# Mirrored filter rows by a DRAM scratch buffer in a spectral filter and token MLP kernel

## The chip, the cores and the metric

The kernel runs on one core of a Trainium2 chip. The metric is the device time of one execution in microseconds; the median of several runs is compared. The engines named below are TensorE (PE, with its weight loads PEld), VectorE (DVE), ScalarE (ACT) and SyncE (SP), whose queue issues nearly all DMA transfers. A DMA transfer is spread over up to 16 DMA engines.

## What is computed

Two branches work on the same input x (2048 rows of 512) and are mixed by a gate per row. Branch A is a two-dimensional Fourier filter: transform, product with a complex weight W of 2048 x 257, back transform. Branch B is a layer norm and an MLP over the rows.

```python
def _A_ref(x, w_r, w_i):
    X = rfft2(x.astype(float32))            # S = 2048 rows, D = 512
    X = X * (w_r + 1j * w_i)                # (2048, 257) each
    return irfft2(X, s=(S, D)).astype(bfloat16)

def _B_ref(x, w1, b1, w2, b2):
    h = _layernorm(x)
    u = gelu(einsum("bsd,sf->bdf", h, w1) + b1)          # F = 1792
    return transpose(einsum("bdf,fs->bds", u, w2) + b2)

g = sigmoid((x * gate_w).sum(-1, keepdims=True))
out = g * A + (1 - g) * B
```

## The kernel before

The kernel is one stream of tasks. `Plan` holds each task with its engine, an estimated duration, what it reads and writes, and a priority. `Plan.order()` runs through the tasks once, on the host, with a clock of its own: at each moment every engine takes, of its tasks that are ready by that clock, the one with the lowest priority number. A DMA task is charged its issue time, then 1.0 us, then its bytes at 388 KB a us, then 0.9 us to land; it waits for the landing of the eighth DMA task before it, and SP is held to 5 us before the end of what it has issued. The order that comes out is emitted as it stands, so each engine of the chip runs a fixed order of its own; only semaphores decide when.

The MLP branch fills PE. L705 (`m1`) multiplies h by w1 in 14 column tiles of F: tiles 0 to 6 from `wa`, 7 to 10 and 11 to 13 from two `wb` buffers, over 16 row tiles each. L721 on ACT is the gelu. L1011 (`m2`) multiplies by w2, which is loaded into `wa` and `wb` once their last w1 tile is used; L1017 on ACT and L1024, L1030 on DVE put the output together.

The Fourier branch is woven in between. L554 to L557 and L653 are its forward matrix products, copied out of PSUM by ACT (L560, L660). DVE does the butterflies: L585 to L598 (`radix4`) and L669 to L677 (`tb2`), each L653 group for half of the second block needing L597 and L598 of that block. L828 multiplies by the filter `W`, L833 to L846 combine; L890 to L898 and L967 to L970 on PE are the way back.

`W` is a tile [128, 2 components, 2 blocks `lt`, 4, 2, 258]. Index 0 of the last but one dimension holds rows of the weight in rising order, index 1 the mirrored rows, in falling order over the partitions. For the real and the imaginary component in turn, `ld_W` (L433) issues 16 SP loads:

- four into `wt` (L439 to L442), which hold the rows of block 0 to be mirrored, in rising order;
- four for block 1, L444, each 128 rows whose source is read as 4 groups of 32, each group backwards;
- four of 32 partitions each, then two for block 0 (63 and 64 partitions), one row of partition 0 and the row `wn`.

Each row is 257 bfloat16 values, 514 bytes. All these DMAs are recorded under L306, the helper `dma`. The four `wb` loads of w1's last columns are issued between the two components.

The `wt` rows are then turned on PE: `wf` (L754) multiplies the permutation `flip` by two of them at a time into a PSUM bank (L757), and ACT copies the result into `W` (L761, 512 columns at a time). The last column, 256, is turned for all at once by L767 and copied by L770. `flip` is also used by L685 for a bias.

`wprep` (L775 to L781) on DVE halves one row of `W` and forms sums of its end columns. It has priority 1, needs all of `W`, and every reader of `W` comes behind it. DVE's butterflies around it have priorities 2.5 to 3.3.

SP's DMAs use eight semaphores in turn: an issue waits until the eighth DMA before it has landed. The loads of w2 stand on SP behind the filter's.

Of the kernel before, what the change touches and what calls it, by code (L numbers as in the profile page):

```python
# [13 lines left out]
BF16 = mybir.dt.bfloat16  # L14
F32 = mybir.dt.float32

P = 128
# [5 lines left out]
L = 256  # L23
WL = 258
# [108 lines left out]
class Plan:  # L133
# [11 lines left out]
    def add(self, eng, dur, emit, reads=(), writes=(), prio=0.0, alloc=(), free=(), nbytes=0, after=(), late=0.0):  # L145
        t = Task()
        t.late = late
        t.eng, t.dur, t.emit, t.prio = eng, dur, emit, prio
        t.alloc, t.free, t.nbytes = tuple(alloc), tuple(free), nbytes
        t.users, t.end, t.ready = [], None, 0.0  # L150
        deps = set(after)
        for k in reads:
            if k in self.last_w:
                deps.add(self.last_w[k])
            self.readers.setdefault(k, []).append(t)
        for k in writes:
            if k in self.last_w:
                deps.add(self.last_w[k])
            deps.update(self.readers.get(k, ()))
            self.last_w[k] = t  # L160
            self.readers[k] = []
        deps.discard(t)
        t.deps = deps
        self.tasks.append(t)
        return t
# [73 lines left out]
def tt(n):  # L239
    return 0.07 + n / 1920.0  # L240
# [10 lines left out]
def act(n, ptr=0):  # L251
    return 0.065 + 0.09 * ptr + n / 1200.0


def mm(*ns):
    return sum(max(n, 120) / 2400.0 + 0.0025 for n in ns)
# [8 lines left out]
def kernel(  # L265
# [14 lines left out]
    V, A, T = nc.vector, nc.scalar, nc.tensor  # L280
# [6 lines left out]
    w2v = B_w2.rearrange("(t f) s -> f t s", f=P)  # L287

    pool = ctx.enter_context(tc.tile_pool(name="sb", bufs=1))
    psum = ctx.enter_context(tc.tile_pool(name="ps", bufs=1, space=bass.MemoryType.PSUM))  # L290
    NES = 2

    def sb(shape, dt, tag, bufs=1):
        return pool.tile(shape, dt, tag=tag, name=tag, bufs=bufs)

    def ps(shape, dt, tag, bufs):
        return psum.tile(shape, dt, tag=tag, name=tag, bufs=bufs)
# [4 lines left out]
    add = pl.add  # L302
    t = {}

    def dma(out_ap, in_ap, eng=None):
        (eng or nc.sync).dma_start(out=out_ap, in_=in_ap)  # L306

    def alloc_first():
        t["eps"] = sb([P, 1], F32, "eps")
        V.memset(t["eps"][:], 1e-5)  # L310
        t["x"] = sb([P, 4, 4, D], BF16, "x")
        t["h"] = sb([P, 4, 4, D], BF16, "h")
        t["X"] = sb([P, 2, 4, 2, 4, P], BF16, "X")
        t["B"] = sb([P, 2, 4, 4, L], BF16, "B")
        t["xp"] = sb([P, 8192], BF16, "xp")
        t["warm"] = t["xp"][:, 0:D]
        V.memset(t["warm"], 0.0)  # L317
        t["s9"] = sb([P, D], BF16, "s9")
        t["b1b"] = sb([P, P], BF16, "b1b")
        t["b2h"] = sb([P, 4, 4], BF16, "b2h")  # L320
        for k in ("s9", "b1b"):
            V.memset(t[k][:], 0.0)
        t["st"] = sb([P, 4096], BF16, "st")
        t["gl"] = sb([P, NFT, D], BF16, "gl")
        t["W"] = sb([P, 2, 2, 4, 2, WL], BF16, "W")
        t["wn"] = sb([1, 2, WL], BF16, "wn")
        t["ta"] = sb([P, 4, 640], BF16, "rot")
        t["wt"] = sb([P, 2, 4, WL], BF16, "wt")
        t["wpm"] = sb([P, 2, 2, 4, 2], F32, "wpm")
        t["sp"] = sb([P, 4, 2, 4], F32, "sp")  # L330
        t["sd"] = sb([P, 2, 2, 2, 4], F32, "sd")
        t["fx"] = sb([P, 4, 2, 4], F32, "fx")
        t["c0"] = sb([P, 2, 4, 2, 2], F32, "c0")
        t["cm"] = sb([P, 4, 4, 2], F32, "cm")
        t["ce"] = sb([P, 2, 4, 2, 2], F32, "ce")
        for name, shape in (("stats", [P, NJ, nc.vector.BN_STATS_DIM]), ("mv", [P, NJ, nc.vector.BN_AGGR_DIM]),
                            ("rstd", [P, NJ]), ("nmr", [P, NJ]), ("glog", [P, NJ]), ("g", [P, NJ]), ("omg", [P, NJ]),
                            ("ombb2", [P, NJ]), ("b1f", [P, NFT])):
            t[name] = sb(shape, F32, name)

    a0 = add("SP", 0.01, alloc_first, writes=["warm", "xs", "eps"], prio=-9)
# [88 lines left out]

    wsrc = (A_w_r, A_w_i)

    def ld_W(comp):  # L433
        v = wsrc[comp].rearrange("(e c k) l -> c e k l", e=4, k=4)
        z = wsrc[comp].rearrange("(v u w) l -> w u v l", v=4, u=2)

        def emit():
            W, u = t["W"][:, comp], t["wt"][:, comp]
            dma(u[64:127, :, 0:257], v[65:128, :, 0, :])  # L439
            dma(u[0:64, :, 0:257], v[64:128, :, 2, :])  # L440
            dma(u[127:128, 0:2, 0:257], z[0:1, 1, 2:4, :])
            dma(u[127:128, 3:1:-1, 0:257], z[0:1, 0, 0:4:3, :])  # L442
            for e in range(4):
                dma(W[:, 1, e, 1, 0:257], v[:, 3 - e, 3, :].rearrange("(o i) l -> o i l", o=4)[:, ::-1])  # L444
            for o in range(4):
                dma(W[32 * o:32 * o + 32, 1, :, 0, 0:257], v[96 - 32 * o:128 - 32 * o, :, 1, :])
            dma(W[1:64, 0, :, 0, 0:257], v[1:64, :, 0, :])
            dma(W[64:128, 0, :, 0, 0:257], v[0:64, :, 2, :])
            dma(W[0:1, 0, :, 0, 0:257].rearrange("w (u v) l -> w u v l", u=2), z[0:1, :, 0:2, :])
            dma(t["wn"][:, comp, 0:257], wsrc[comp][1024:1025, :])  # L450
        return emit

    for comp in range(2):
        add("SP", 12.3, ld_W(comp), writes=[("W", comp), ("wt", comp)], prio=17 + 8 * comp, nbytes=300000, after=[a0])
        if comp == 0:
            load_wb(1)

# [14 lines left out]
    for r in range(4):  # L472
# [3 lines left out]
        for b, qs in enumerate(groups):  # L476
            js = [4 * q + r for q in qs]
            xb = [xk[q] for q in qs]
            g = (r, b)
# [5 lines left out]
            for j in js:  # L485
# [10 lines left out]
                if j in ASTAT:  # L496
# [4 lines left out]
                    after=[rect[0, 0]] if j == 4 else ())  # L501
# [23 lines left out]
            for j in js:  # L525
                if j in HACT:
                    add("ACT", 0.71, lambda j=j: A.activation(t["h"][:, j // 4, j % 4, :], t["x"][:, j // 4, j % 4, :], ActF.Identity,  # L527
                                                                  bias=t["nmr"][:, j:j + 1], scale=t["rstd"][:, j:j + 1]),
                        reads=xb + [("rstd", *g)] + mvk, writes=[("h", j)], prio=-0.5 + 0.1 * r)
# [19 lines left out]
        for dq in range(4):  # L549
            def fa(r=r, dq=dq):  # L550
# [8 lines left out]
                free=["xf"] if dq == 3 else ())  # L559
            add("ACT", act(512), lambda r=r, dq=dq: A.copy(xe(r)[:, :, :, dq, :], t["pa", r, dq][:]),  # L560
                reads=[("pa", r, dq)], writes=[("X", r, dq)], prio=0, free=["fa"])
# [69 lines left out]
    for lt in (0, 1):  # L631
        pr = 3.0 + 0.1 * lt
# [3 lines left out]
        if lt == 0:  # L636
            add("DVE", 0.15, lambda: V.tensor_copy(t["X"][:, 0, :, :, :, 0], t["fx"][:]), reads=["fx"],
                writes=[("Z", 0, 0), ("Z", 0, 1)], prio=3.0)
# [76 lines left out]
    for n, (ft, j) in enumerate(order):  # L715
# [4 lines left out]
        if last:  # L720
# [3 lines left out]
                free=[bank]))  # L724
# [21 lines left out]

    add("SP", 0.2, ld_ti, writes=["ti"], prio=39, nbytes=754176, after=[pl.last_w["pa", r, dq] for r in range(4) for dq in range(4)])

    for comp in range(2):
        for lt in (0,):  # L750
            for a in range(2):
                tag = ("fa", "fb")[a]

                def wf(comp=comp, lt=lt, a=a, tag=tag):  # L754
                    pw = t["pw", comp, lt, a] = ps([P, 2, L], F32, tag, 2)
                    for i in range(2):
                        T.matmul(pw[:, i], lhsT=t["flip"][:], rhs=t["wt"][:, comp, 3 - 2 * a - i, 0:L], start=True, stop=True)  # L757
                add("PE", mm(256, 256), wf, reads=[("wt", comp), "flip"], writes=[("pw", comp, lt, a)], prio=5, alloc=[tag])

                def wfe(comp=comp, lt=lt, a=a):  # L760
                    A.copy(t["W"][:, comp, lt, 2 * a:2 * a + 2, 1, 0:L], t["pw", comp, lt, a][:])  # L761
                add("ACT", act(512), wfe, reads=[("pw", comp, lt, a)], writes=[("W~", comp, lt)], prio=3, free=[tag])

    def wfn():
        pw = t["pwn"] = ps([P, 4, 2], F32, "fa", 2)
        for e in range(4):
            T.matmul(pw[:, e], lhsT=t["flip"][:], rhs=t["wt"][:, :, 3 - e, 256], start=True, stop=True)  # L767
    add("PE", mm(*[4] * 4), wfn, reads=[("wt", 0), ("wt", 1), "flip"], writes=["pwn"], prio=5, alloc=["fa"])
    wtk = [("W~", comp, 0) for comp in range(2)]
    add("ACT", 0.3, lambda: A.copy(t["W"][:, :, 0, :, 1, 256], t["pwn"][:].rearrange("p e k -> p k e")),  # L770
        reads=["pwn"], writes=wtk, prio=3, free=["fa"])

    pbk = [("pb", lt, e, c) for lt in range(2) for e in range(4) for c in range(2)]

    def wprep():  # L775
# [3 lines left out]
        pv = [pm[:, i].rearrange("p a e k -> p (a e) k") for i in range(2)]  # L779
        V.tensor_add(pv[0], ends[0][:, :, 0], ends[0][:, :, 1])  # L780
        V.tensor_sub(pv[1], ends[1][:, :, 0], ends[1][:, :, 1])  # L781
    add("DVE", 0.8, wprep, reads=[], writes=[("W", 0), ("W", 1), "wpm"] + wtk, prio=1)


    for lt in range(2):
# [37 lines left out]
        for comp in range(2):  # L823
            def mul(lt=lt, comp=comp):
                xs = xph(0).rearrange("p (k c l) -> p k c l", k=8, c=2)
                o = (xph(1) if comp == 0 else t["st"][:]).rearrange("p (k c l) -> p k c l", k=8, c=2)
                w = t["W"][:, comp, lt].rearrange("p e s l -> p (e s) l")[:, :, None, 0:L].to_broadcast([P, 8, 2, L])
                V.tensor_mul(o, xs, w)  # L828
            add("DVE", tt(4096), mul, reads=["xs", ("W", comp), ("W~", comp, lt)], writes=[("pp", "st")[comp]], prio=pr)

        def comb(lt=lt):
            y, pp, qq = (v.rearrange("p (k c l) -> p k c l", k=8, c=2) for v in (xph(0), xph(1), t["st"][:]))
# [246 lines left out]
```

## Time and profile before

| what | value |
|---|---|
| median of 3 runs | 127.81 us (127.77 to 128.35) |
| the profiled execution | 127.68 us |
| its span, first to last instruction | 125.9 us |
| PE busy | 120.5 us, 96% of the span |
| DVE busy | 113.8 us, 90% |
| ACT busy | 81.0 us, 64% |
| DMA moved | 23.12 MB, mean 184 GB/s |
| granted TensorE clock | 1.0 throughout |

The span is cut into 40 slices of 3.15 us. A digit is the busy share of a slice in tenths:

```profile
PE   6899999999999999999999999999999999999991
ACT  0973689699999999999420004722299999952200
DMA  1999999994459946799999900000000000006541
GB/s 57 305 371 358 382 365 358 348 315 86 117 119 288 268 86 162 210 413 411 410 408 407 389 25 0 5 0 0 3 0 0 0 5 0 0 21 229 200 180 44
```

In a timeline, a row is start, duration, engine (SPq is SP's queue), line, operation, the tiles written and read, and how many were merged; an idle time before it and what ended it stand in brackets. In the list of waits, a row is the waiting engine and line, what it waited for, and the total in us, the number of waits and the longest. A window row is its bounds and length, the busy time of PE, PEld, DVE, ACT and POOL with the number of instructions, the granted clock, the mean busy share of the 16 DMA engines and GB/s. The trace also holds a landing mark for each DMA engine that takes part in a transfer.

### The profile page before, as it was taken

The page shows a single profiled execution, that of the slowest core. Times are in us where ns is not written, and L with a number is a line of the kernel's source. Part 1 is how long each engine was busy: PE and PEld are TensorE (multiplying, and loading weights), DVE is VectorE, ACT ScalarE, POOL GpSimd, SP SyncE. Part 2 cuts the span into 40 slices and gives each one's busy share as a digit, 9 for nine tenths or more (in the row PEclk, how much of TensorE's full clock was granted, in tenths as well). Part 3 has the DMA queues.
Part 4 walks back from the last instruction along what each step waited for, and adds up shares of the span by engine and source line. Part 5 has one row for each costly group of instructions (what it writes and reads, how often), then busy time and mean ns, then how long its engine had stood idle before and what let it go on. Part 6 is the DMA issues. An engine that isn't in the chain of part 4 may idle for free.

```text
span 125.9 us, 2138 instructions
## 1 busy us (share of the span) xinstructions
PE 120.5 (96%) x743; PEld 68.8 (55%) x756; DVE 113.8 (90%) x273; ACT 81.0 (64%) x165; POOL 0.2 (0%) x4
## 2 busy tenths in 40 slices
PE   6899999999999999999999999999999999999991
PEld 2344555555655476644445555555577767655590
DVE  2699999999999999999999999999988999999651
ACT  0973689699999999999420004722299999952200
POOL 0000000000000000000000000000000000000000
PEclk9999999999999999999999999999999999999999
DMA  1999999994459946799999900000000000006541
GB/s 57 305 371 358 382 365 358 348 315 86 117 119 288 268 86 162 210 413 411 410 408 407 389 25 0 5 0 0 3 0 0 0 5 0 0 21 229 200 180 44
DMA packets 18219, 23.12 MB, mean 184 GB/s; under 512 B 2190, under 2 KB 15904, under 8 KB 18208
## 3 DMA queue, kind: packets, MB, share of 16 engines
q1 hardware_dynamic: 17616, 22.36, 52.6%
q10 hardware_dynamic: 592, 0.62, 1.6%
q8 instruction: 6, 0.10, 0.3%
q14 instruction: 5, 0.04, 0.1%
HBM read 20.86 MB, written 2.10 MB: 182 GB/s over the span
## 4 chain that ended last, share of the span: by engine, by line
PE 73%; DMA 17%; SPq 7%; issue 1%; DVE 0%
PE acc L1011 32%; PE acc L705 20%; DMA wa<-in_B_w_dram 9%; SPq L306 7%; PE fb L1011 5%; DMA wt<-in_A_w_r_dram 5%; DMA x<-in_A_x_dram 3%; PE fb L653 2%; PE fa L653 2%; PE fa L890 2%; PE fb L890 1%; PE fb L705 1%; PE fa L967 1%; PE fb L967 1%; PE fa L1011 1%
## 5 line engine op out<-in xcount | busy, mean ns | idle before, releaser
L705 PE MATMUL acc<-h,wb 128*128 128x512 bf16 x108 | 25.9, 379 | 0.1
L1011 PE MATMUL acc<-gl,wb 128*128 128x512 bf16 (+1 forms) x94 | 23.9, 371 | 0.2
L1011 PE MATMUL acc<-gl,wa 128*128 128x512 bf16 (+1 forms) x97 | 23.8, 371 | 0.1
L1017 ACT ACTIVATE x<-acc,ombb,omg 128x512 bf16<-128x512 f32 x12 | 9.1, 782 | 21.2 <-PE acc L1011 21.2
L1011 PEld LDWEIGHTS <-wa 128*128 128x128 bf16 x126 | 13.5, 113 | 9.9
L1011 PEld LDWEIGHTS <-wb 128*128 128x128 bf16 x126 | 13.3, 113 | 9.3
L705 PE MATMUL acc<-h,wa 128*128 128x512 bf16 x62 | 17.3, 379 | 0.1
L705 PEld LDWEIGHTS <-wb 128*128 128x128 bf16 x112 | 10.7, 98 | 10.6
L705 PEld LDWEIGHTS <-wa 128*128 128x128 bf16 x112 | 10.3, 98 | 10.7 <-DMA wa<-in_B_w_dram 0.8
L487 DVE BATCH_NORM_STATS2 stats<-x 128x6 f32<-128x512 bf16 x14 | 9.5, 679 | 2.1 <-DMA x<-in_A_x_dram 2.0
L560 ACT CAST xp<-fa 128x512 bf16<-128x512 f32 x16 | 9.1, 581 | 1.8 <-PE fa L557 1.8
L735 ACT ACTIVATE x<-x 128x512 bf16<-128x512 bf16 x16 | 10.2, 691 | 0.0
L721 ACT ACTIVATE gl<-acc,b1f 128x512 bf16<-128x512 f32 x11 | 7.9, 718 | 3.2 <-PE acc L705 3.2
L705 PE MATMUL fb<-h,wa 128*128 128x512 bf16 x31 | 9.5, 379 | 0.1
L527 ACT ACTIVATE h<-x,nmr,rstd 128x512 bf16<-128x512 bf16 x11 | 8.4, 808 | 1.1 <-DMA wb<-in_B_w_dram 0.8
L705 PE MATMUL fa<-h,wa 128*128 128x512 bf16 x16 | 5.9, 378 | 0.7 <-DVE h L521 0.6
L653 PEld LDWEIGHTS <-X 128*128 128x128 bf16 x64 | 4.7, 98 | 2.1
L974 ACT ACTIVATE B<-fb,g 128x512 bf16<-128x512 f32 x8 | 5.7, 713 | 0.0
L974 ACT ACTIVATE B<-fa,g 128x512 bf16<-128x512 f32 x8 | 5.6, 705 | 0.1
L660 ACT CAST X<-fb 128x512 bf16<-128x512 f32 x8 | 5.1, 634 | 0.0
L660 ACT CAST X<-fa 128x512 bf16<-128x512 f32 x8 | 5.0, 620 | 0.0
L356 PE MATMUL fa<-xp 128*128 128x512 bf16 x10 | 3.8, 549 | 1.2 <-DVE xp L317 1.2
(169 smaller groups left out, 232.7 us busy)
## 6 DMA issues: line engine op xcount, KB each, us to landing
wb<-in_B_w_dram SPq DMA_DIRECT2D x11, 512.0 KB
wa<-in_B_w_dram SPq DMA_DIRECT2D x7, 512.0 KB
wa<-in_B_w_dram SPq DMA_DIRECT2D x2, 896.0 KB
wb<-in_B_w_dram SPq DMA_DIRECT2D x4, 384.0 KB
out_dram<-x SPq DMA_DIRECT2D x3, 512.0 KB
x<-in_A_x_dram SPq DMA_DIRECT2D x2, 512.0 KB
wa<-in_B_w_dram SPq DMA_DIRECT2D x2, 448.0 KB
rot<-dft_ti SPq DMA_DIRECT2D x1, 768.0 KB
```

What stands on the lines that cost most here:

```text
L306: (eng or nc.sync).dma_start(out=out_ap, in_=in_ap)
L487: V.bn_stats(out=t["stats"][:, j, :], in_=t["x"][:, j // 4, j % 4, :])
L527: add("ACT", 0.71, lambda j=j: A.activation(t["h"][:, j // 4, j % 4, :], t["x"][:, j // 4, j % 4, :], ActF.Identity, bias=t["nmr"][:, j:j ...
L560: add("ACT", act(512), lambda r=r, dq=dq: A.copy(xe(r)[:, :, :, dq, :], t["pa", r, dq][:]), reads=[("pa", r, dq)], writes=[("X", r, dq)], ...
L653: T.matmul(pb[:, k % 2, k // 2], lhsT=t["X"][:, lt, EX[e], c, k, :], rhs=tbl(k, c), start=True, stop=True)
L660: A.copy(t["X"][:, lt, EX[e]].rearrange("p c j l -> p (c j l)").rearrange("p (h c g b) -> p h c g b", h=2, c=2, b=2)[:, :, c], t["pb", lt, ...
L705: T.matmul(t["u", ft][:], lhsT=w[:, j // 4, j % 4, c * P:(c + 1) * P], rhs=t["h"][:, j // 4, j % 4, :], start=(j == jorder[0]), stop=(j == ...
L721: gelus.append(add("ACT", act(512, 1) , lambda ft=ft: A.activation(t["gl"][:, ft, :], t["u", ft][:], ActF.Gelu_apprx_tanh, bias=t["b1f"][: ...
L735: A.activation(t["x"][:, q, r, :], t["x"][:, q, r, :], ActF.Copy, accum_out=t["glog"][:, 4 * q + r:4 * q + r + 1])
L974: A.activation(eo_v(p)[:, n], t["i3", j][:], ActF.Copy, scale=t["g"][:, j:j + 1])
L1011: T.matmul(t["y", j, m][:, cs], lhsT=w[:, o, 512 * q + r:512 * q + 512:4], rhs=t["gl"][:, ft, cs], start=(ft == 0), stop=(ft == NFT - 1))
L1017: A.activation(tbuf(j).rearrange("p h d -> p (h d)"), t["y", j, 0][:], ActF.Identity, bias=t["ombb2"][:, j:j + 1], scale=t["omg"][:, j:j + 1])
```

## The change

The mirrored rows no longer pass through `wt`, PE and ACT. For each component, `ld_flip` issues two copies from the weight in DRAM into scratch buffers in DRAM, `fe` (4 x 128 rows) and `fo` (16 x 32 rows), each with its second dimension read backwards. `ld_nat` issues the loads in rising order, ten for each component, among them two single rows that need no turning. `ld_mir` reads the scratch buffers back into `W` with three loads for each component. The task durations given to the planner are 1.1 us for `ld_flip` (with 700,000 bytes), 5.5 for `ld_nat` (300,000) and 1.6 for `ld_mir` (500,000); by priority, SP's order is both `ld_flip`, `ld_nat` of the first component, the four `wb` loads, `ld_nat` of the second, both `ld_mir`, then w2. The tile `wt` and the tasks `wf`, `wfe` and `wfn` (L749 to L771) go, which the diff below leaves out; `wprep` waits for the four loads' tasks.

```diff
+    dram = ctx.enter_context(tc.tile_pool(name="dram", bufs=1, space=bass.MemoryType.DRAM))
...
-        t["wt"] = sb([P, 2, 4, WL], BF16, "wt")
...
-    def ld_W(comp):
+    def ld_flip(comp):
+        ev = wsrc[comp].rearrange("(e m w) l -> w e m l", e=4, w=2)[0, :, P:2 * P, :]
+        od = wsrc[comp].rearrange("(g i k) l -> k g i l", i=32, k=4)[3]
+
+        def emit():
+            fe = t["fe", comp] = dram.tile([4, P, 257], BF16, tag=f"fe{comp}", name=f"fe{comp}")
+            fo = t["fo", comp] = dram.tile([16, 32, 257], BF16, tag=f"fo{comp}", name=f"fo{comp}")
+            dma(fe[:], ev[:, ::-1])
+            dma(fo[:], od[:, ::-1])
+        return emit
+
+    def ld_nat(comp):
         v = wsrc[comp].rearrange("(e c k) l -> c e k l", e=4, k=4)
         z = wsrc[comp].rearrange("(v u w) l -> w u v l", v=4, u=2)
 
         def emit():
-            W, u = t["W"][:, comp], t["wt"][:, comp]
-            dma(u[64:127, :, 0:257], v[65:128, :, 0, :])
-            dma(u[0:64, :, 0:257], v[64:128, :, 2, :])
-            dma(u[127:128, 0:2, 0:257], z[0:1, 1, 2:4, :])
-            dma(u[127:128, 3:1:-1, 0:257], z[0:1, 0, 0:4:3, :])
-            for e in range(4):
-                dma(W[:, 1, e, 1, 0:257], v[:, 3 - e, 3, :].rearrange("(o i) l -> o i l", o=4)[:, ::-1])
+            W = t["W"][:, comp]
             for o in range(4):
                 dma(W[32 * o:32 * o + 32, 1, :, 0, 0:257], v[96 - 32 * o:128 - 32 * o, :, 1, :])
             dma(W[1:64, 0, :, 0, 0:257], v[1:64, :, 0, :])
             dma(W[64:128, 0, :, 0, 0:257], v[0:64, :, 2, :])
             dma(W[0:1, 0, :, 0, 0:257].rearrange("w (u v) l -> w u v l", u=2), z[0:1, :, 0:2, :])
+            dma(W[0:1, 0, 0:2, 1, 0:257], z[0:1, 0, 0:4:3, :])
+            dma(W[0:1, 0, 3:1:-1, 1, 0:257], z[0:1, 1, 2:4, :])
             dma(t["wn"][:, comp, 0:257], wsrc[comp][1024:1025, :])
         return emit
 
+    def ld_mir(comp):
+        def emit():
+            W, fe, fo = t["W"][:, comp], t["fe", comp], t["fo", comp]
+            m = fe[:].rearrange("e (p two) l -> two p e l", two=2)
+            dma(W[:, 1, ::-1, 1, 0:257], fo[:].rearrange("(e o) i l -> (o i) e l", e=4))
+            dma(W[1:64, 0, ::-1, 1, 0:257], m[1, 0:63])
+            dma(W[64:128, 0, ::-1, 1, 0:257], m[0, 0:64])
+        return emit
+
+    FL = (16, 16.1)
     for comp in range(2):
-        add("SP", 12.3, ld_W(comp), writes=[("W", comp), ("wt", comp)], prio=17 + 8 * comp, nbytes=300000, after=[a0])
+        add("SP", 1.1, ld_flip(comp), writes=[("flp", comp)], prio=FL[comp], nbytes=700000, after=[a0])
+    for comp in range(2):
+        add("SP", 5.5, ld_nat(comp), writes=[("W", comp)], prio=17 + 8 * comp, nbytes=300000, after=[a0])
+        add("SP", 1.6, ld_mir(comp), reads=[("flp", comp)], writes=[("W~", comp)], prio=26 + comp, nbytes=500000)
         if comp == 0:
             load_wb(1)
...
-    add("DVE", 0.8, wprep, reads=[], writes=[("W", 0), ("W", 1), "wpm"] + wtk, prio=1)
+    add("DVE", 0.8, wprep, reads=[], writes=[("W", 0), ("W", 1), ("W~", 0), ("W~", 1), "wpm"], prio=1)
```

## The prediction

> **What bounds the kernel now.** I read the page first (busy times, slices, chain of waits), then the timelines of DVE, PE and SyncE's queue (SP) around the changed work, then SP's waits and a few windows.
>
> ```profile
> PE 120.5 (96%) x743; PEld 68.8 (55%) x756; DVE 113.8 (90%) x273; ACT 81.0 (64%) x165; POOL 0.2 (0%) x4
> DVE  2699999999999999999999999999988999999651
> PE 73%; DMA 17%; SPq 7%; issue 1%; DVE 0%
> ...
> 24.90 2.56 SPq L306 DMA_DIRECT2D wt<-in_A_w_r_dram  x4
> 27.95 7.55 SPq L306 DMA_DIRECT2D W<-in_A_w_r_dram  x11
> 36.01 2.62 SPq L306 DMA_DIRECT2D wb<-in_B_w_dram  x4
> 41.27 8.55 SPq L306 DMA_DIRECT2D W<-in_A_w_i_dram  x11
> 50.40 3.30 SPq L306 DMA_DIRECT2D wa<-in_B_w_dram  x7
> ...
> SPq L306 <- DMA wb<-in_B_w_dram: 4.4, 4, 1.5
> ...
> 31.60:32.60 1.00, 1.00 (x11) 0.81 (x10) 1.00 (x2) 1.00 (x3) 0.00 (x0) 1.00 0.22 58
> ...
> 46.68 0.68 DVE L591 TENSOR_TENSOR X<-xp 128x1024 bf16<-128x1024 bf16 x1
> 47.55 0.69 DVE L669 TENSOR_TENSOR B<-X 128x1024 bf16<-128x1024 bf16 x1 [0.18 <-ACT X L660]
> 48.83 0.68 DVE L597 TENSOR_TENSOR X<-st 128x1024 bf16<-128x1024 bf16 x1
> 57.46 0.41 DVE L777 TENSOR_SCALAR W<-W 1x1028 bf16<-1x1028 bf16 x1
> ...
> 38.65 0.38 PE L757 MATMUL fa<-wt,flip 128*128 128x256 bf16 x2
> 53.02 0.38 PE L757 MATMUL fa<-wt,flip 128*128 128x256 bf16 x2
> ```
>
> TensorE sets the end (96% busy), but DVE is packed too: one slice after another at 9. Both run a fixed order, so a wait put into one of them in mid kernel is not filled by later work. SP is not free either: from 24.9 to 50.3 us it does nothing but issue filter loads, with the four `wb` loads between.
>
> **How an order comes to be.** The planner fixes every engine's order by its own due times; the chip then waits in that order. I take from it only where DVE's `wprep` (L777, L780, L781), which needs the whole filter, is put. Its clock can be laid on the trace: it lets the first turning matmul go 0.15 + 0.9 + 300000/388e3 + 1.0 = 2.82 us after `ld_W`'s 12.3 us of issue. The trace has it at 38.65, so the planner's `ld_W` began at 38.65 - 15.1 = 23.5; from the second (53.02) it is 37.9, and 23.5 + 12.3 + 4 x 0.5 = 37.8. The two marks agree.
>
> With the new costs from 23.5: flips 1.1 each, but SP is also held to 5 us before the planner's transfers end (at most 23.5 + 5 = 28.5 beforehand, and 1.8 more for each 700,000 bytes: 32.1), so 27.1; plain loads 5.5, 32.6; `wb` 2.0, 34.6; second plain loads 40.1; mirror reads 1.6 each, 43.3; then 1.0 + 1.29 + 0.9: due at 46.5. `wprep` has priority 1 against 2.5 and 3 of its neighbours, so it goes into DVE's next gap: behind L591, which ends at 47.3, ahead of L669 and L597. Before, it stood behind work that ended at 57.4.
>
> **What the chip does with SP's new queue.** An SP load waits until the eighth before it has landed: in the trace the first turned load is issued at 27.95 after a landing mark at 27.94, the second at 29.96 (29.94), and in the second group at 44.00 (43.98). That is the 4.4 us in the row of waits. The plan charges the new loads 0.55 us each and no such wait; the old 12.3 us for 16 was 0.77 each.
>
> Cost of a scratch row: no DRAM to DRAM copy is in the trace. Nearest rows: the old turned loads L444, 128 rows of 514 bytes whose source is 4 x 32. While they alone run, 0.22 of 16 engines are busy (last window line): 4 engines. Two of them land 1.1 us apart, so 32 rows an engine cost 1.1 us, 34 ns a row. Rows written to DRAM at the end (512 bytes, L306 stores) take 27 ns, rows read into SBUF 28 ns. The lower bound is that both overlap: 34 ns; the upper that they add, 28 + 27 and the same gap of 6 ns: 61 ns. I take 34, since the read rows already include a write.
>
> How many engines: `fo` is 16 x 32 on both sides. `fe` is 4 x 128, and the row with an outer size of 4 ran on 4 engines, so I take 4: 128 rows an engine, 4.4 us; `fo` 32 rows, 1.1 us. The other bound is 16 engines: 1.1 us for all four.
> By the Trainium skill, page "DMA: Bandwidth & Descriptors", section "Why a DMA increments its semaphore by 16 and not by 1", the number of engines is the largest up to 16 that divides the slowest dimension of both sides. By that rule `fe` gets 4 too, as the 0.22 suggests.
>
> Now in order. A load on idle engines (the first `o` load, issued by 32.30) has its first marks at 33.72: 1.4 us to land. The low four engines come free at 28.3 at the latest (old `wt` rows there landed by 30.47, less 1.4 and 28 rows, 0.95 us). Landings: fe0 28.3 + 4.4 + 1.4 = 34.1, fo0 35.2, fe1 39.6, fo1 40.7. The four `o` loads go out by 31.7 as the turned ones did. The fifth plain load waits for fe0 (34.1), the sixth for fo0 (35.2), the seventh for fe1 (39.6), the eighth for fo1 (40.7); two more end at 42.4, against 32.6 in the plan. `wb` 2.6 us (row of 36.01): 45.0. Second plain loads: four by 47.0; the next four wait for the `wb` loads, which before landed 3.4 (first) to 6.9 us (last) after their issue ended: 50.1 to 51.9 for the last, then 1.6: 51.7 to 53.5. Six mirror reads at 0.53: 54.9 to 56.7. Landing 1.4 + 16 rows x 34 ns: 56.8 to 58.6, middle 57.7.
>
> **The sum.**
> - DVE waits at `wprep` from 47.3 to 57.7: +10.4. Behind it stand L669 and L597/L598; L598 feeds the last four L653 groups (51.00 to 52.5 in the chain), and PE, in order, stops there, about 3.5 us after DVE and just as long. Behind that stand all of L1011 and ACT's copies L660. So the wait counts once.
> - Turning matmuls: 4 x 0.22 + 0.08 us of the chain (pieces at 38.81, 39.03, 53.18, 53.40, 53.84) = 0.96 off PE. Those before the stall (0.44) vanish in it; -0.52.
> - ACT copies L761, L770: 0.59 + 0.59 + 0.70 + 0.70 + 0.34 = 2.9 us, -0: ACT is in no piece of the chain. The weight loads of `flip` run under matmuls, -0. `wprep` itself is moved: 0.
> - SP: 32 loads become 30. First `wa` load of w2 at about 55.9 instead of 50.4. The cover is the stall, which moves L1011's start (64.35) by 10. Without it: seven loads of 512 KB at some 410 GB/s (the slices' rate there) take 9 us and land at about 66.4, 2 us of PE waiting.
> - Bytes: 1.05 MB more, while the DMA row of the slices stands at 4 to 7 tenths for half of 28 to 53 us: 0.
>
> 127.68 (profiled execution: span 125.9 and 1.8 around it) + 10.4 - 0.5 = 137.6. The median of the runs shown, 127.81, is 0.13 higher; I leave the forecast at 137.6.
>
> **Rivals.**
> 1. `fe` runs on 16 engines. Then all flips have landed by about 35.3 (slowest engine free at 29.5, 4 x 1.1 + 1.4), plain loads end at 36.7, `wb` 39.3, second plain loads 46.0 to 47.8, mirror reads landed 51.1 to 52.9. Stall 4.7: 131.9. For: no row shows such a copy. Against: the 0.22.
> 2. A DRAM to DRAM row costs 61 ns. fe 7.8, fo 2.0: fo1 lands 8.6 later, stall 19: 146.2. For: nothing here both reads and writes DRAM. Against: 512-byte rows to DRAM at 27 ns.
> 3. Not slower: `wprep` finds its filter there. Place: L777 on DVE. It decides at W's last landing against DVE's turn: if the turn comes 10.4 us later than I work out (the plan puts `wprep` where it was, 57.4), or the mirror rows land by 47.3 (16 engines for `fe`, no wait for a `wb` load: 24.9 + 30 x 0.53 = 40.8 is SP's floor, plus the wait at 29.96 and 2 us to land: 47 to 48). Price: 0.5 to 0.96 gained, 126.7 to 127.2; a wait of up to 1 us makes it no change. For: DVE waited nowhere for the filter before. Against: two marks that agree on the planner's clock, and the waits at 27.95, 29.96 and 44.00.
> 4. The copy doesn't do what it says, by being lowered in small pieces of more packets. It would show as rival 2 or beyond; I count it there.
>
> **How the numbers follow.** Forecast (134 to 142, from landings at 54 to 62) 0.48; rival 1 and stalls partly made good (129 to 134) 0.20; rivals 2 and 4 (142 to 150) 0.17; rival 3 0.15, of which 0.11 faster and 0.04 the same. No change means within 0.5%, 0.64 us, about what a measurement of this kernel can tell. Slower: 0.48 + 0.20 + 0.17 = 0.85. The range 130 to 146 leaves out rival 3 and about a third of the long tail, 0.2. Cases of both signs exist, but the likeliest's own 134 to 142 lies on one side.
>
> **What would show it.** In the changed profile: L777 on DVE near 47, not 57, as it is issued behind L591, with an idle time of some 10 us before it, ended by a DMA into W; the same on PE before a group of L653 near 51; SP rows with gaps before the fifth and the seventh plain load; the DMA busy share near 4 of 16 while the scratch copies run. No turning matmuls, no copies to W on ACT. The landing of fe0 against fo0 gives the row price and the engines. I am wrong if `wprep` runs near 57, or with no idle time before it; if the idle time is there but PE's is much shorter, the step that passes DVE's wait on to PE is wrong.

## The result, and the profile after

The change makes the kernel slower: 144.32 us median of 6 runs (142.21 to 145.29) against 127.79. The ratio of 1.121, with a 95% interval of 1.113 to 1.129, is that of the fast runs alone (142.21, 143.52 and 144.28), the other three being over 1.5% above the fastest. The profiled execution took 142.21 us with a span of 140.4; before, 127.68 and 125.9.

Line numbers shift: the helper of all DMAs is now L307; L591 became L611, L597 L617, L669 L689, L653 L673, L705 L725, L1011 L1007, and `wprep` (L777, L780, L781) is L773, L776, L777.

Page of the changed kernel: busy time of the engines, the slices (40 of 3.5 us), the chain of waits.

```profile
PE 122.7 (87%) x744; PEld 68.9 (49%) x744; DVE 113.5 (81%) x273; ACT 79.2 (56%) x160; POOL 0.2 (0%) x4
PE   6899999999999960007999999999999999999991
DVE  1799999999999401039969999999997999999941
PEclk9999999999999998555699999999999999999999
DMA  3999999953772993999999290000000000005441
PE 52%; DMA 26%; SPq 17%; DVE 2%; issue 1%; DVEq 0%
```

Busy times are nearly those of before; the span is longer because DVE stands still for most of 47 to 62 us and PE from 51 to 64 us, where the rows fall to 0. The granted clock falls to half in the same place. In the chain, PE's share went from 73% to 52%, DMA's and SP's grew from 24% to 43%.

The timeline of SP's queue in the changed kernel:

```profile
24.64 0.75 SPq L307 DMA_DIRECT2D fe<-in_A_w_r_dram  x1
25.44 4.20 SPq L307 DMA_DIRECT2D fo<-in_A_w_r_dram  x1
29.69 0.84 SPq L307 DMA_DIRECT2D fe<-in_A_w_i_dram  x1
30.57 4.20 SPq L307 DMA_DIRECT2D fo<-in_A_w_i_dram  x1
34.81 7.72 SPq L307 DMA_DIRECT2D W<-in_A_w_r_dram  x9
43.03 2.62 SPq L307 DMA_DIRECT2D wb<-in_B_w_dram  x4
45.70 7.17 SPq L307 DMA_DIRECT2D W<-in_A_w_i_dram  x9
53.37 0.65 SPq L307 DMA_DIRECT2D W<-fo  x1
54.07 1.55 SPq L307 DMA_DIRECT2D W<-fe  x2
55.66 0.62 SPq L307 DMA_DIRECT2D W<-fo  x1
56.33 1.44 SPq L307 DMA_DIRECT2D W<-fe  x2
57.87 3.77 SPq L307 DMA_DIRECT2D wa<-in_B_w_dram  x7
```

The mirror reads begin at 53.37, when the old queue had already issued all its filter loads and six of the first seven weight loads of w2 (the seventh at 53.27). W2's first load goes out at 57.87 instead of 50.40. By the landing marks the last mirror read is there at 62.01; the last filter load of before landed at 52.02.

The timelines of DVE and of PE in the changed kernel, in brackets the idle time before the instruction and what ended it:

```profile
46.68 0.69 DVE L611 TENSOR_TENSOR X<-xp 128x1024 bf16<-128x1024 bf16 x1
53.88 0.42 DVE L773 TENSOR_SCALAR W<-W 1x1028 bf16<-1x1028 bf16 x1 [6.51 <-DMA W<-in_A_w_i_dram]
59.40 0.18 DVE L776 TENSOR_TENSOR wpm<-W 128x16 f32<-128x16 bf16 x1 [5.10 <-DMA W<-fo]
62.09 0.19 DVE L777 TENSOR_TENSOR wpm<-W 128x16 f32<-128x16 bf16 x1 [2.51 <-DMA W<-fe]
62.19 0.69 DVE L689 TENSOR_TENSOR B<-X 128x1024 bf16<-128x1024 bf16 x1
...
50.19 1.24 PE L725 MATMUL acc<-h,wb 128*128 128x512 bf16 x5
64.21 0.61 PE L673 MATMUL fa<-tb,X 128*128 128x128 bf16 x4 [12.78 <-DVE X L617]
66.06 4.20 PE L725 MATMUL acc<-h,wb 128*128 128x512 bf16 x12
```

`wprep` now runs right behind L611, ahead of L689 and L617, and waits three times: 6.51 + 5.10 + 2.51 = 14.1 us. PE stops at 51.43 and waits 12.78 us for L617. Then it works at half speed for a while, as a window of the changed kernel shows (bounds and length, busy time and count of PE, PEld, DVE, ACT and POOL, granted clock, DMA share, GB/s):

```profile
64.20:69.20 5.00, 4.99 (x24) 2.76 (x25) 5.00 (x17) 2.26 (x5) 0.00 (x0) 0.52 1.03 410
```

A clock of 0.52 over 5.0 us is 2.4 us of work not done. The profiled executions differ by 142.21 - 127.68 = 14.5 us: 12.8 us of PE's waiting, 2.4 of slow clock, less 0.96 of turning matmuls that are gone, make 14.2; 0.3 stays unassigned.

### The profile page after: what moved, and what is told of

It reads as the page before. It is cut to its first block, busy times and chain, and to the rows that moved or that the text cites. A ratio compares the mean times of both kernels' runs of the same rounds, so it can differ in the third digit from the quotient of the medians.

```text
span 140.4 us, 2117 instructions
## 1 busy us (share of the span) xinstructions
PE 122.7 (87%) x744; PEld 68.9 (49%) x744; DVE 113.5 (81%) x273; ACT 79.2 (56%) x160; POOL 0.2 (0%) x4
## 4 chain that ended last, share of the span: by engine, by line
PE 52%; DMA 26%; SPq 17%; DVE 2%; issue 1%; DVEq 0%
PE acc L1007 29%; SPq L307 17%; PE acc L725 9%; DMA fo<-in_A_w_i_dram 8%; DMA wa<-in_B_w_dram 7%; PE fb L1007 5%; DMA wb<-in_B_w_dram 5%; DMA W<-fe 3%; DMA x<-in_A_x_dram 3%; PE fa L886 1%; PE fb L886 1%; PE fa L673 1%; PE fb L673 1%; PE fa L963 1%; PE fb L963 1%
## 5 line engine op out<-in xcount | busy, mean ns | idle before, releaser
L725 PE MATMUL acc<-h,wb 128*128 128x512 bf16 x112 | 27.3, 394 | 0.0
L1007 PE MATMUL acc<-gl,wb 128*128 128x512 bf16 (+1 forms) x98 | 24.2, 372 | 0.0
L1007 PE MATMUL acc<-gl,wa 128*128 128x512 bf16 (+1 forms) x98 | 23.8, 372 | 0.0
L1007 PEld LDWEIGHTS <-wa 128*128 128x128 bf16 x126 | 13.4, 114 | 9.9
L1007 PEld LDWEIGHTS <-wb 128*128 128x128 bf16 x126 | 13.3, 113 | 9.4
L725 PE MATMUL acc<-h,wa 128*128 128x512 bf16 x64 | 17.6, 379 | 0.0
L725 PEld LDWEIGHTS <-wb 128*128 128x128 bf16 x112 | 11.1, 102 | 12.4 <-issue 1.6
L725 PEld LDWEIGHTS <-wa 128*128 128x128 bf16 x112 | 10.3, 98 | 10.7 <-DMA wa<-in_B_w_dram 1.0
L673 PE MATMUL fa<-tb,X 128*128 128x128 bf16 x32 | 3.6, 242 | 12.8 <-DVE X L617 12.8
L673 PEld LDWEIGHTS <-X 128*128 128x128 bf16 x64 | 4.9, 109 | 15.2 <-DVE X L617 13.3
L725 PE MATMUL fb<-h,wa 128*128 128x512 bf16 x32 | 9.7, 379 | 0.0
L725 PE MATMUL fa<-h,wa 128*128 128x512 bf16 x16 | 5.9, 379 | 0.7 <-DVE h L541 0.6
L773 DVE TENSOR_SCALAR W<-W 1x1028 bf16<-1x1028 bf16 x1 | 0.4, 421 | 6.5 <-DMA W<-in_A_w_i_dram 6.5
```

The source lines that it names most:

```text
L673: T.matmul(pb[:, k % 2, k // 2], lhsT=t["X"][:, lt, EX[e], c, k, :], rhs=tbl(k, c), start=True, stop=True)
L725: T.matmul(t["u", ft][:], lhsT=w[:, j // 4, j % 4, c * P:(c + 1) * P], rhs=t["h"][:, j // 4, j % 4, :], start=(j == jorder[0]), stop=(j == ...
L1007: T.matmul(t["y", j, m][:, cs], lhsT=w[:, o, 512 * q + r:512 * q + 512:4], rhs=t["gl"][:, ft, cs], start=(ft == 0), stop=(ft == NFT - 1))
```

## The experiments

Five questions: what the place of `wprep` costs, what lies under its wait, whether the slow clock is real time, what the copies cost and through which resource, and what the removal is worth by itself.

**e1: `wprep` put back, nothing else.**

```diff
-        add("SP", 1.6, ld_mir(comp), ..., prio=26 + comp, nbytes=500000)
+        add("SP", 1.6, ld_mir(comp), ..., prio=26 + comp, nbytes=500000, late=15.5 * comp)
```

> The changed kernel with one figure more for the planner: the mirror reads of the imaginary component are said to land 15.5 us later. No transfer changes; on DVE wprep moves from right behind the second radix-4 pair to the place behind the g/omg operations, just ahead of the product with W. Theory (the fixed order puts wprep too early and DVE, then PE, wait in order): DVE's 14.1 us and PE's 12.8 us of waiting go, the granted clock stays at 1.0 throughout, W still lands near 62. What is left is that the w2 loads are issued 7 us later than before (57.9 against 50.4), which PE has to wait for at about 64 to 70: 130 to 135 us, 1.02 to 1.06 of the kernel before. Rival (the late filter and its transfers set the end, wherever wprep stands): 139 us or more, with the wait moved to the new place.

Measured 139.69 us (138.20 to 140.51): a miss of the theory, and inside the rival's 139 or more. Timelines of e1, DVE and PE:

```profile
62.12 0.19 DVE L776 TENSOR_TENSOR wpm<-W 128x16 f32<-128x16 bf16 x1 [2.45 <-DMA W<-fo]
65.11 0.19 DVE L777 TENSOR_TENSOR wpm<-W 128x16 f32<-128x16 bf16 x1 [2.80 <-DMA W<-fe]
...
65.95 0.41 PE L1007 MATMUL acc<-gl,wa 128*128 128x512 bf16 x1 [1.80 <-DMA wa<-in_B_w_dram]
68.52 0.62 PE L1007 MATMUL acc<-gl,wa 128*128 128x512 bf16 x1 [0.87 <-DMA wa<-in_B_w_dram]
72.04 0.62 PE L1007 MATMUL acc<-gl,wa 128*128 128x512 bf16 x1 [1.62 <-DMA wa<-in_B_w_dram]
```

The long wait near 47 is gone and DVE now waits 5.3 us near 60. But w2's first weights were issued only at 60.60, and PE eats them as they land, one matmul at a time (L1007, 7.3 us of waiting in seven pieces, the clock falling to half at 67.89: 0.41 becomes 0.62 us a matmul). A second cost of the change had been covered by the first.

**e2: `fo` padded to 33 rows, read back in four loads.** It was to show whether the shape of `fo`'s destination, which can be merged into one long run, makes its issue take 4.20 us.

> The changed kernel with the scratch buffer fo padded to 33 rows a group, so that both sides of its copy keep the shape 16 x 32, and with its mirror read cut into four loads of 32 partitions (six more SP loads). Theory: SP's 4.2 us of issue for each fo copy come from the two sides having different shapes, and fall to 0.5 to 0.8 us, 7 us less for SP; but the seventh plain load still waits for the second fe copy (landed near 40), so SP is no earlier from there, and W's last landing stays at 61 to 64: 142 to 146 us. Rival (SP's issue time is what makes the filter late): W lands 4 to 7 us earlier and the time falls to 136 to 139. If the 4.2 us belong to any DRAM to DRAM copy on 16 engines, they stay.

Measured 145.42 us (145.04 and 145.81), and `fo` still took 3.99 and 4.42 us to issue. The shape of its destination is not it.

**e3, e5, e6: TensorE kept busy through the wait.** 56 (e3) or 74 (e5) matmuls whose result nobody uses stand ahead of the last L673 groups; e6 is the change once more, beside e5.

```diff
+    def busy():
+        pw = ps([P, D], F32, "fa", 2)
+        for _ in range(74):
+            T.matmul(pw[:], lhsT=t["tb"][:, 0:P], rhs=t["tb"][:, P:P + D], start=True, stop=True)
+    add("PE", 0.01, busy, reads=["tb"], writes=["busy"], prio=1.95, ..., after=[pl.last_w["pb", 1, 2, 1]])
```

> The changed kernel with 56 matmuls of 128x512 more, whose result nobody reads, put on PE just ahead of where it waits. Theory (PE idle for 12.8 us loses its clock, and works at half speed for some 4.8 us after the wait, 2.4 us lost): the granted clock stays 1.0, the groups behind the wait take 0.39 instead of 0.61 us, and the time is 2.0 to 2.6 us less than the changed kernel's, 139.5 to 142. Rival (the lower clock costs nothing because PE waits for others there anyway): the clock stays up and the time does not change, 142 to 145.

> The change with 74 matmuls of 128x512 (0.4 us each by e3's groups, some 16 us with their weight loads' share as in e3, where 56 took 12) put on TensorE right ahead of its wait, results unused; nothing else is touched. Theory: of the change's loss 2.4 us are the granted clock at 0.5 after 13 idle us, so with TensorE kept busy the clock stays at 1.0 through the filter's stage and the time is 1.5 to 2.4 us under the change's own, run beside it as e6. Rival: the clock's fall is paid by nobody, since the first groups after the wait are paced by DVE anyway: within 0.5 us of e6. If the added matmuls outlast the wait the time would rise with them.

> The change unaltered, for comparison with e5, e7 and e8 on one chip: 142 to 145 us, as before.

e3: 143.87 us (140.88 to 144.98), inconclusive: its 56 matmuls were too few, PE still waited 3.35 us for L617's result, and the clock fell all the same, from 68.53 to 71.94. e5: 144.25 (143.31 to 145.22); e6: 145.43 (144.17 to 147.21). The medians of e5 and e6 differ by 1.2 us (0.4 without e6's two longest runs), less than expected and too little to decide, because the filter's landing differs between executions by more than the effect: in e6's profiled execution `wprep` got its last rows at 66.37, in the first profile of the change at 62.09. Measured from that moment to the end of the span the effect is plain: 140.4 - 62.09 = 78.3 for the change, 145.0 - 66.37 = 78.6 for e6, and 142.2 - 65.92 = 76.3 for e5. The slow clock costs 2.0 to 2.3 us, by one profile of each. Three more profiles agree: behind the wait PE works at half speed for 5.3 us in e6, 4.8 in the change, 4.1 in e9, 3.4 in e3, 3.1 in e2 and not at all in e5, and the way to the end is 78.6, 78.3, 78.0, 78.0, 77.5 and 76.3 us. Windows of e5 over the 5 us behind the wait:

```profile
68.00:73.00 5.00, 4.80 (x35) 2.59 (x35) 5.00 (x17) 4.04 (x10) 0.00 (x0) 1.00 1.04 414
```

35 matmuls in the same 5 us in which the change did 24.

**e4: the removal alone.** The kernel before without turning and its copies; `wt`'s four loads go straight into `W` in rising order, which leaves part of the filter unmirrored.

> The kernel before with the turning taken out alone: the mirrored rows of block 0 are loaded straight into W by the same SP loads, in rising order, so that part of the filter is not mirrored. No scratch buffer, the same 32 SP loads, no matmuls by flip for the filter, no ACT copies into W. It prices what the change removes. Theory: 0.5 to 1.0 us less than the kernel before (0.96 us of matmuls leave a PE that is 96% busy, ACT's 2.9 us are cover): 126.8 to 127.3, ratio 0.992 to 0.996. Rival (ACT's copies or DVE's wait for them matter too): 125.5 or less. Other rival: nothing, since DVE is as full as PE: 127.6 to 128.

126.91 us (126.70 to 127.32), ratio 0.993 (0.991 to 0.996). So by this run all that the change can win here is 0.8 us.

**e7: the change with true durations in the plan.**

```diff
-        add("SP", 1.1, ld_flip(comp), ...)
+        add("SP", 5.0, ld_flip(comp), ...)
-        add("SP", 5.5, ld_nat(comp), ...)
-        add("SP", 1.6, ld_mir(comp), ...)
+        add("SP", (9.4, 8.9)[comp], ld_nat(comp), ...)
+        add("SP", 2.2, ld_mir(comp), ..., late=1.5)
```

> The change with three of its planned durations set to those in its own trace (a pair of scratch copies 5.0 instead of 1.1, the plain loads 9.4 and 8.9 instead of 5.5, the mirror reads 2.2 instead of 1.6, and their landing 1.5 later); no transfer, no instruction is added or taken away, only the order on the engines can differ. Theory (two costs of nearly the same size, one hidden under the other): DVE no longer waits before L611's follow-up, but the second layer's first weights are still issued at 57 to 60 and TensorE waits at L1007 instead: 136 to 140 us, as e1. Rival (the planned durations were the whole loss): 127 to 131 us.

135.0 us (133.61 to 135.49), 9.3 less than the change and 10.4 less than e6 beside it, between the two. DVE has no long wait near 47. PE keeps 45 matmuls of L725 for the gap, as in e1; but, told that w2 comes late, it then takes seven output tiles at a time at L1007 (groups of four, two and one matmul from 66.80 on), where e1 took one and waited for the next weights, and it waits 2.1 us instead of 7.3. What stays: DVE's idle times near 60, in e7's timeline

```profile
59.37 0.17 DVE L761 TENSOR_SCALAR omg<-g 128x16 f32<-128x16 f32 x1 [2.07 <-ACT g L757]
62.98 0.19 DVE L776 TENSOR_TENSOR wpm<-W 128x16 f32<-128x16 bf16 x1 [2.80 <-DMA W<-fo]
66.01 0.19 DVE L777 TENSOR_TENSOR wpm<-W 128x16 f32<-128x16 bf16 x1 [2.85 <-DMA wa<-in_B_w_dram]
...
126.70 0.55 PE L1007 MATMUL fb<-gl,wb 128*128 128x128 bf16 x7
129.95 0.34 DVE L1020 SCALAR_TENSOR_TENSOR x<-fb,omg,x 128x128 bf16<-128x128 f32 x1
```

7.7 us in all, and DVE's product with the filter (L824, which was L828) begins at 69.35 instead of 62.01. At the end PE is done at 127.25, 4.2 us later than before (its wait at L1007, 0.9 us for a load of `wb`, and a clock at half from 67.67 to 71.09), and DVE works on to 130.3, another 3 us: DVE now holds the end (13% of e7's chain, against none before). The releaser named for L777 is a load of w2 that landed in the same moment; the filter's own last mark is at 65.94.

**e8: the copies issued from GpSimd**, behind a two-element read of a loaded `wb` tile (`dma(fe[:], ev[:, ::-1], nc.gpsimd)`, same for `fo`).

> The change with its four scratch copies issued from GpSimd's queue behind a two-element copy that waits for the first block of wb (landed 24.7), and the plan told 8.0 and 9.0 us for the plain loads and 2.2 us later landing of the mirror reads. The bytes and rows that move are the same. Theory (SP's queue carries the loss: the copies hold it for 10 us): SP comes to the second layer's weights at 46 to 50 us, where the kernel before had 50.4, wprep stands later on DVE, and the time is 126.5 to 129 us. Rival (the 16 engines are full, the copies only move their queue): the mirror reads wait for copies that land late, the second layer's weights stand behind them on SP, 134 us or more.

136.19 us median (133.51 to 137.48), close to the rival's 134 or more. As e8's plan also puts `wprep` late, its neighbour is e7 with 135.0 and not the change: moving the copies to another queue gained nothing. SP is free of the copies, and its queue in e8 reads

```profile
24.63 8.67 SPq L307 DMA_DIRECT2D W<-in_A_w_r_dram  x9
33.81 11.01 SPq L307 DMA_DIRECT2D wb<-in_B_w_dram  x4
55.43 3.88 SPq L307 DMA_DIRECT2D wa<-in_B_w_dram  x6
```

Four `wb` loads take 11.01 us to issue instead of 2.62: the plain loads ahead of them land up to 43.97, because the DMA engines are busy with the copies, and each issue waits for the eighth before. The filter is complete at 61.44, hardly earlier than the change's 62.01. The Trainium skill has this as a rule, on page "DMA: Bandwidth & Descriptors", section "Rules for kernel authors": spreading DMAs over several issuing engines saves issue time and adds no bandwidth, since they share the 16 DMA engines. This run agrees.

**e9, e10: `fe` on 16 engines.** `fe` is written as 128 x 4 rows in rising order (part of the filter stays unmirrored); e10 has e7's durations besides.

```diff
-            fe = t["fe", comp] = dram.tile([4, P, 257], ...)
-            dma(fe[:], ev[:, ::-1])
+            fe = t["fe", comp] = dram.tile([P, 4, 257], ...)
+            dma(fe[:], ev.rearrange("e m l -> m e l"))
```

> The change with fe written row by row in rising order, rows outermost, so that its 512 rows go to 16 engines instead of 4; the mirror reads take them from there (this leaves part of the filter unmirrored). Bytes, rows, loads and order of issue are those of the change. Theory (four engines hold up everything behind them): a copy of fe takes each of them 128 rows at some 34 ns, 4.4 us, and would take 32 rows, 1.1 us; two copies give 6.6 us back to the loads queued behind, so the wait for the filter falls from 14 to 7 or 9 us and the time to 135 to 138 us. Rival (issuing is the bound, some 10 us on SP whatever the engines do): both copies of fo keep their 4.2 us of issue, and the time stays within 1.5 us of the change's 142 to 145.

> e9 with the planned durations of e7, so that DVE comes to the filter later (part of the filter stays unmirrored). If e7's remaining loss of 7 us is weights of the second layer that come late behind full engines, giving 6.6 us back leaves 0 to 2.5 us of loss: 128 to 130.5 us. If it is instructions put in a worse order by the other plan, it stays at 133.5 to 135.5.

e9: 140.95 us (140.43 to 142.79); e10: 130.59 (130.14 to 130.80). SP's queue in e9:

```profile
24.72 1.28 SPq L307 DMA_DIRECT2D fe<-in_A_w_r_dram  x1
26.05 1.41 SPq L307 DMA_DIRECT2D fo<-in_A_w_r_dram  x1
27.51 1.38 SPq L307 DMA_DIRECT2D fe<-in_A_w_i_dram  x1
28.93 1.21 SPq L307 DMA_DIRECT2D fo<-in_A_w_i_dram  x1
```

`fo`, unchanged, is issued in 1.41 and 1.21 us instead of 4.20: its long issue came from standing behind `fe`. That four crowded engines are what matters in `fe` is likely but not separated from the order of its rows, which e9 changes too. The rival's reason is refuted, as `fo` did not keep its 4.2 us; its time, within 1.5 us of 142 to 145, is nevertheless the one that came, and the theory's 135 to 138 was missed. Of the 4.6 us that SP gained here, the end of the last mirror read's issue kept 1.0 (56.76 against 57.77) and the filter 0.8 (61.24): the second group of plain loads waits for `wb` loads that land no earlier than 48.4 and 50.6. So the copies did run faster on 16 engines, and little of it reached the filter: the time fell by 3.4 us of median, by 1.1 between the profiled spans. e10 lies 0.1 above the range expected. With the filter at 62.77 instead of e7's 65.94, PE waits 0.27 us at L1007 instead of 2.14, its clock stays up, and it is done at 123.0, as in the kernel before. What is left is e7's tail:

```profile
62.85 0.19 DVE L777 TENSOR_TENSOR wpm<-W 128x16 f32<-128x16 bf16 x1 [2.71 <-DMA W<-fe]
...
122.44 0.55 PE L1007 MATMUL fb<-gl,wb 128*128 128x128 bf16 x7
125.71 0.34 DVE L1020 SCALAR_TENSOR_TENSOR x<-fb,omg,x 128x128 bf16<-128x128 f32 x1
```

DVE's product with the filter begins at 66.19, still 4.2 us later than before, and DVE ends 3 us behind PE (0.4 us before).

**e11, e12: no copies.** The mirror reads take the same rows from the weight itself, in rising order (part of the filter unmirrored); e12 has measured durations besides.

```diff
-            dma(fe[:], ev[:, ::-1])
-            dma(fo[:], od[:, ::-1])
+            t["fe", comp], t["fo", comp] = ev, od
```

> The change without the four scratch copies: the mirror reads take the same rows from the filter in HBM itself, in rising order (this leaves part of the filter unmirrored); issue order, DVE's order and the planned durations stay. Theory (the copies are the whole loss, the mirror reads themselves are cheap): SP is 10 us ahead, the filter is there at 50 to 52, DVE waits 3 to 5 us, the second layer's weights are issued at 47 to 50: 128.5 to 132 us. Rival (the mirror reads, 152 rows on each of the four lowest engines, some 6 us, are as dear): the filter lands at 55 or later and the time is 135 us or more.

> e11 (mirror reads from the filter in HBM, no copies, part of the filter unmirrored) with the planned durations as measured: copies nothing, plain loads 8.8 and 9.4, mirror reads 2.2 with a landing 2.5 later, so that DVE comes to the filter behind L757 of this kernel's g and not right behind the first radix stage. Theory: e11's whole loss of 7.7 us is the early place of wprep on DVE, against a filter that lands 3 us later than in the kernel before; with the place put back and the second layer's weights issued at 50.2 as before, nothing is left: 126.5 to 128 us. Rival (the mirror reads on the DMA engines delay the second layer's weights too): 129 us or more, with TensorE waiting at L1007 of the change (here some lines up).

e11: 135.39 us (135.19 to 136.62), where its rival had it. Without any copy the last mirror read is issued by 50.12 and lands at 54.96, and `wprep`, still right behind the first butterflies, waits 4.27 + 3.01 us; PE waits 5.85 us behind it and then works at half clock for 5.1. e12: 127.12 us (126.75 to 127.63), ratio 0.994 (0.991 to 0.996). Its timeline of DVE (lines three lower: `wprep` is L770, L773, L774):

```profile
57.29 0.17 DVE L694 COPY B<-X 128x4 bf16<-128x4 bf16 x1
57.37 0.41 DVE L770 TENSOR_SCALAR W<-W 1x1028 bf16<-1x1028 bf16 x1
57.81 0.19 DVE L773 TENSOR_TENSOR wpm<-W 128x16 f32<-128x16 bf16 x1
```

No idle time stands before any of the three. The filter landed at 56.49, 1.5 us later than in e11, and costs nothing. So here the mirror reads are free once DVE comes at 57.37, where the kernel before had `wprep` too (57.46).

The four kernels side by side, medians in us:

| | `wprep` early, as the change plans it | durations as measured, `wprep` late |
|---|---|---|
| with the copies | 144.3 | 135.0 |
| without the copies | 135.4 | 127.1 |

Each of the two causes costs about 8 to 9 us whether or not the other is there, and with both gone the 0.8 us of e4 remains. The step from left to right is the whole plan, on every engine: `wprep`'s place alone, in e1, was worth 4.6 us. The step from top to bottom is the copies with all that they hold up: `fe` on 16 engines accounts for 3.4 us of it on the left (e9) and 4.4 on the right (e10), and how the rest divides was not tested. No version that mirrors the whole filter came below the kernel before; the nearest is e7.

## Why the prediction was right, and where it fell short

**Where `wprep` goes** was right: behind L611, 46.68 to 47.37 in the trace, and DVE's wait begins there. The reading of the planner's clock from the two marks held.

**How the copies run** was right: fe0 landed at 34.40 (worked out 34.1), fo0 at 35.26 (35.2), fe1 at 40.52 (39.6), fo1 at 41.25 (40.7). `fe` left four marks at its end, `fo` sixteen. Between the landings of fe0 and fe1, 160 rows on each of the four engines took 6.12 us, 38 ns a row against the 34 taken. The way to the first group's end was partly luck. "The four `o` loads go out by 31.7 as the turned ones did" failed: the copies' issue had been priced like that of plain loads, `fo` took 4.20 us each time, and the four were out by 37.45. The fifth and sixth (37.50 and 37.90) waited for no copy, as fe0 and fo0 had long landed. It cost nothing only because the seventh (40.53) had to wait for fe1 (40.52) in any case. Rival 1 fell in its premise, and e9 adds that it would have won less than it said (140.95 where the rival had 131.9). Rival 2 fell as well: its band of 142 to 150 holds the result, but not for its reason, as fe0 would have landed at 37.5. Rival 3 named the point from which no loss follows, a turn at 57 with the filter there, and e12, without the copies, stands at that point, at the price it gave (126.7 to 127.2).

**The steps that failed by size.** The wait was 14.1 us, not 10.4. The second group of plain loads ended at 53.32, inside the 51.7 to 53.5 worked out, 0.7 above its middle. The rest is the step "Six mirror reads at 0.53 ... Landing 1.4 + 16 rows x 34 ns": the issue took 4.4 us instead of 3.2, and the last landed 4.2 us after its issue instead of 1.95. I counted the rows of the last read alone. The six overlap and share engines: 32 + 28 + 16 rows, twice, are 152 rows on an engine that takes part in all, and their packets run in the trace from 54.8 to 60.9 us, 6.1 us, 40 ns a row. So their own rows, more than the last issue, set the landing; in the last 2 us w2's first loads share the engines with them. 0.7 + 1.2 + 2.3 = 4.2 us, which carries 57.7 to 61.9.

The second missing term is the clock. PE's wait was there, 12.8 us, somewhat less than DVE's, since L617's result had come 1.5 us ahead of its use before. That PE then works at half speed for 4.8 us was nowhere in the sum, a term put at nothing without a reason; e5 puts it at 2.0 to 2.3 us. The Trainium skill's page "TensorE: Matmul & The Clock Gate", Part 1, "The HAM clock gate", says that the clock falls to half after an idle window of about 3.4 us and needs as long of work to come back. In the trace both took somewhat longer: it fell 3.9 us after PE stopped (51.43 to 55.32) and rose 4.8 us after it went on (64.21 to 68.98). A wait need not last as long as the 3.4 us of the Trainium skill, and there the measurement decides: in e3 the clock fell after a wait of 3.35 us and in e7 after one of 2.14, both times with PE already at work again.

Together: the profiled execution is 4.6 us above the 137.6 forecast, 2.4 from PE's longer wait (12.8 against 10.4), 2.4 from the clock, less 0.4 because the turning saved 0.96 and not 0.52, with the 0.3 unassigned. The median lies 2.1 us higher still: the profiled execution was the fastest of the six.

**The cover.** The shift of w2 was costed at nothing under the stall, which was right for this kernel (PE has no wait over 0.15 us behind 64.21), and at "2 us of PE waiting" without it. There e1 shows 7.3 us of waiting and 139.7 us: its weights were issued at 60.60, not 55.9, and they run into a full set of DMA engines, so the first lands 5.3 us after issue. Small as it looked, this term is why undoing the first cause alone wins little.

The turning was priced nearly right: 0.96 in all, 0.52 of it outside the stall; e4 gives 0.8 in all.

## What to carry to other kernels

Work out when the last of a group of transfers lands from all the rows that the group puts on its busiest DMA engine, not from the last transfer. When a stall is predicted, ask what else became late under it and price that as if the stall were gone: here two causes of 8 to 9 us each lay one behind the other. Where a planner orders the work, wrong durations are themselves a cost: correcting three durations and one landing time was worth 9 to 10 us with no transfer changed.

## What the runs showed of the hardware

- A copy from DRAM to DRAM whose outer size is 4 ran on 4 engines, at 34 to 38 ns for a row of 514 bytes. The next DMA's issue was slow: 4.20 us for `fo` behind `fe` on 4 engines, 1.41 and 1.21 behind `fe` on 16 (with its rows in rising order). What in the queue holds the issue back was not seen.
- The TensorE clock of these traces is 1.0 or 0.5, and its low stretches in mid kernel last 3.41 us (e3, e7), 6.83 (e11), 10.24 (e1, e8), 13.66 (the change, e9) or 17.07 (e2, e6): whole multiples of 3.41. Waits of 0.65 to 1.80 us between single matmuls did not keep it up: in e1 it stayed at half from 67.89 to 78.13.
- With the copies the kernel varies more from run to run: the change ranged from 142.2 to 147.2 us, the kernel before from 127.7 to 128.9. Two profiles place it in the landing of the filter (62.01 and 66.29 us), not in the engines' work. Why it lands 4 us later in one execution was not settled.
